# Stage B of a spectral filter on 64x32 and 32x64 array tiles, with each filter row stored once

## The chip, the core and the metric

One core of one Trainium2 chip runs the whole program. It has TensorE (PE, matmuls, which reads SBUF and writes PSUM), VectorE (DVE), ScalarE (ACT), GpSimd (POOL), SyncE (SP, here only an issuer of DMAs) and 16 DMA engines that all issuers share. PSUM has eight banks of 128 x 512 fp32. The metric is the device time of one execution in microseconds (us); it is the same for every engine, and the last engine to finish sets it.

## The reference

```python
def _attn_ref(x, filt_r, filt_i):          # x (8, 3008, 256), filters (1505, 256)
    X = np.fft.rfft(x, axis=1)
    Y = X * (filt_r + 1j * filt_i)[None, :, :]
    return np.fft.irfft(Y, n=x.shape[1], axis=1).astype(np.float32)

def _moe_ref(x, w_gate, w_val, w_out):     # x (24064, 256), d_ff 1536
    gate = np.maximum(x @ w_gate, 0.0)
    val = x @ w_val
    return (gate * val @ w_out).astype(np.float32)
```

The output of the first is the input of the second. All inputs and the output are fp32.

## The kernel before, in words

**The transform.** The 3008 positions of a batch are split as 94 x 32. Stage A transforms along the 94 (a matmul with a constant matrix; `a_0` and `a_1` for batches 0 and 1, `tiled_a` on 32x32 array tiles for batches 2 to 7). Stage B transforms along the 32, multiplies by the filter and transforms back along the 32. Stage C (`item_c`) transforms back along the 94 and yields `yT`, 512 tokens at a time. Then comes the feed-forward part (`gv`, `o_part`).

**Stage B before.** The 48 row groups of a batch are handled in six steps i. `fwd(b, i)` issues 8 matmuls on 64x64 array tiles (four at once) into two PSUM banks psX; `product(b, i, e, k)` multiplies one bank by the real filter (k = 0, result `tt`) or the imaginary one (k = 1, result `uu`) on DVE; in batch 0, eight of the `uu` are made on POOL from a copy `xs` that ACT takes out of PSUM first. `inv(b, i)` issues 16 matmuls on 64x64 tiles into two banks psD, with constant tables I2t for `tt` and I2u for `uu`; ACT copies both banks out (DVE one in batch 0). The result goes to DRAM (`Dbuf`), in batch 0 to SBUF. A 64-row tile holds the real parts of a group in 32 rows and the imaginary parts in 32 more, and both halves are multiplied by the same filter row: the filter tables Ftr and Fti (24 groups x 256) hold each row twice. The tables are loaded by POOL's DMAs (`load_filters`), and `place_filter` then copies 32 rows to the other 32, seven times by DMAs on SP's queue and once by POOL. Tables I2t come out of F2 by small matmuls (`make_back_t`), I2u out of I2t by a matmul with a swap matrix (`make_back_u`), with a few rows from a constant (`place_own`).

**The order of work.** It is written by hand; every engine runs its instructions in the order in which the program issues them. PSUM banks come from a first-in first-out list (`bank`, `done`), fixed when the program is built. The prologue is: x of batch 0 on the SP and ACT queues; filters on POOL, held back by `hold_gpsimd` until the first half of x is in; stage A of batch 0 (12 items after the first four), with the tables made beside the last of them; `first_b`, which is stage B of batch 0 with `amid(i)` between the steps (warm-up matmuls and `make_back_u` at i < 3, a stage-A item of batch 1 after that); the rest of stage A of batch 1. SP issues the filter copies, and x of batch 1 among and behind them.

Then come 47 blocks of 512 tokens, each of 12 steps. Step ft (its position in the block, 0 to 11) is `gv` (psV and psG, two matmuls each; ACT casts psV to `vsb`, DVE makes `prod` of psG and `vsb`), `o_part` of the block before (four psO matmuls, ACT's copy `osb` at positions 5 and 11), then whatever `at_step` has put on this step, then at positions 8 and 10 `item_c` of the next block, one half each. The half of position 8 is cast to `yT` by ACT, that of position 10 by DVE. The next block's first psV needs the first half for its first matmul and the second half for its second. `at_step` spreads the batches' work: for batch b, `end` is the step (always position 3) before whose neighbourhood its stage C begins, and the offsets in the code count from it. `turn_1(k)` are three DVE transposes of batch 1 in the first two blocks.

Of the kernel before, what the change touches and what calls it, by code (L numbers as in the profile page):

```python
# [40 lines left out]

def _tables():
# [9 lines left out]
    own = np.zeros((128, 2, 2, 64))  # L52
    for hg in range(48):
        g, a = divmod(hg, 2)
        rows = slice(a * 64, a * 64 + 64)
        e, j = g % 2, 12 * a + g // 2
# [4 lines left out]
        k1 = 1 + g + 24 * a if hg != 47 else 0  # L61
        th = 2 * np.pi * (((n1 - 23) * k1) % N1) / N1
        wa[part, rt] = np.cos(th)
        if k1 not in (0, 47):
# [5 lines left out]
            conj = np.tile([1.0, -1.0], 16)  # L70
# [3 lines left out]
            ct, st = c.T, s.T  # L74
            t[:] = np.block([[ct, st], [-st, ct]])
            u[:] = np.block([[-st, ct], [-ct, -st]]) * np.concatenate([conj, conj])[:, None]
        else:
# [9 lines left out]
            if k1 == 0:  # L87
                sign = np.where(n2 % 2 == 0, 1.0, -1.0)
                f[0:32, 32] = sign
                t[0, 0:32] = 1.0  # L90
                t[32, 0:32] = sign
                u[0] = 0.0
                u[32] = 0.0
        f2[lo + 64 * e, j] = f
        if g >= NG - 2:
            own[rows, 0, g - NG + 2], own[rows, 1, g - NG + 2] = t, u
# [4 lines left out]
    swap = np.zeros((128, 128))  # L101
    conj = np.where(r % 2 == 0, 1.0, -1.0)
    swap[r ^ 32, r] = conj * np.where(r & 32, -1.0, 1.0)
    fold = np.zeros((128, 4, 32))
    i = np.arange(24)
    for odd in range(2):
        k1 = 2 - odd + 2 * (i % 12) + 24 * (i // 12)
        if not odd:
            k1[k1 == 48] = 0
        th = 2 * np.pi * (np.outer(i - 23, k1) % N1) / N1  # L110
        half = np.where(i == 23, 0.5, 1.0)[:, None]
        for q in range(4):
            fold[32 * q:32 * q + 24, 2 * odd, 0:24] = np.cos(th) * half
            fold[32 * q:32 * q + 24, 2 * odd + 1, 0:24] = np.where(k1 % 47 == 0, 0.0, -np.sin(th))
    tab = np.concatenate([perm, swap, own.reshape(128, -1), m1.reshape(128, -1)], 1)
# [4 lines left out]
def kernel(  # L120
# [57 lines left out]
    I2t = consts.tile([128, NG, 64], BF16)  # L178
    I2u = consts.tile([128, NG, 64], BF16)
    Ftr = consts.tile([128, NG, D], BF16)  # L180
    Fti = consts.tile([128, NG, D], BF16)
# [18 lines left out]
    perm, swap = tabs[:, 0:64], tabs[:, 64:192]  # L200

    def make_back_t(q):

        psI = [bank("psI", 4, 64) for _ in range(2)]
        for e in range(2):
            for a in range(2):
                for j in range(4):
                    nc.tensor.matmul(psI[e][64 * a:64 * a + 64, j],
                                     F2[64 * e:64 * e + 64, 12 * a + 4 * q + j, :],
                                     perm[64 * e:64 * e + 64], start=True, stop=True,  # L210
                                     tile_position=(64 * e, 64 * a))
        for e in range(2):
            nc.scalar.copy(I2t[:, 8 * q + e:8 * q + 8:2, :], psI[e])
            done(psI[e])

    def make_back_u(q):

        psI = bank("psI", 8, 64)
        nc.tensor.matmul(psI, swap, I2t[:, 8 * q:8 * q + 8, :], start=True, stop=True)
        nc.scalar.copy(I2u[:, 8 * q:8 * q + 8, :], psI)  # L220
        done(psI)

    def place_own():

        for i, t in enumerate((I2t, I2u)):
            o = 192 + i * 128
            nc.gpsimd.tensor_copy(t[64:, NG - 2:, :],
                                  tabs[64:, o:o + 128].rearrange("p (g n) -> p g n", g=2))

    nyq = []  # L230

    def load_filters():

        for g0 in (0, H):
            for src, dst in FILT:
                for a in range(2):
                    r, k1, n = a * 64, 1 + 24 * a + g0, H - (2 * a if g0 else 0)
                    nc.gpsimd.dma_start(dst[r:r + 31:2, g0:g0 + n, :],
                                        _ap(src, k1 * D, [[N1 * D, 16], [1, n * D]]))
                    nc.gpsimd.dma_start(dst[r + 1:r + 32:2, g0:g0 + n, :],  # L240
                                        _ap(src, (N1 - k1) * D, [[N1 * D, 16], [-D, n], [1, D]]))
            yield

    def load_own_filters():
        for src, dst in FILT:
            nc.gpsimd.dma_start(dst[64:95:2, NG - 2:, :],
                                _ap(src, 47 * D, [[N1 * D, 16], [-47 * D, 2], [1, D]]))
            nyq.append(pro.tile([1, D], BF16, tag="nyq", bufs=2, name="nyq"))
            nc.gpsimd.dma_start(nyq[-1], _ap(src, (S // 2) * D, [[D, 1], [1, D]]))

    def place_filter(fi, a, half, copy):

        dst = FILT[fi][1]
        gs = slice(H * half, H * half + H)
        r = a * 64
        copy(dst[r + 32:r + 64, gs, :], dst[r:r + 32, gs, :])

    def place_nyq():
        for (src, dst), n in zip(FILT, nyq):
            nc.gpsimd.tensor_copy(dst[96:97, NG - 1, :], n)  # L260
# [141 lines left out]
    psXs, tus, dsbs, left = {}, {}, {}, {}  # L402
    CUTS = (0, 2, 4, 6)

    def fwd(b, i):
# [4 lines left out]
        for m in range(2):  # L410
            for e in range(2):
                for a in range(2):
                    j = 12 * a + 2 * i + m
                    nc.tensor.matmul(psXs[b, i, e][64 * a:64 * a + 64, m],  # L414
                                     F2[64 * e:64 * e + 64, j, :],
                                     ats[b][64 * e:64 * e + 64, j, :] if b > 1 else ats[b][64 * e:64 * e + 64, :, j, :],
                                     start=True, stop=True, tile_position=(64 * e, 64 * a))

    def product(b, i, e, k, pool=False):

        psX = psXs[b, i, e]
        pool_, bufs = (fs, 4) if b else (pro, 6)
        p = pool_.tile([128, 2, D], BF16, tag=("tt", "uu")[k], bufs=bufs, name=("tt", "uu")[k])
        filt = (Ftr, Fti)[k][:, 4 * i + e:4 * i + 4:2, :]
# [11 lines left out]
    def inv(b, i):  # L436

        if b and i in CUTS:
            dsbs[b] = i, sb.tile([128, 2, 4, D], BF16, tag="dsb", bufs=3, name="dsb")
        psD = [bank("psD", 2, D) for a in range(2)]  # L440
        for m in range(2):
            for k in range(2):
                for a in range(2):
                    for e in range(2):
                        nc.tensor.matmul(psD[a][64 * e:64 * e + 64, m],  # L445
                                         (I2t, I2u)[k][64 * a:64 * a + 64, 4 * i + 2 * m + e, :],
                                         tus[b, i, e, k][64 * a:64 * a + 64, m],
                                         start=(k == 0), stop=(k == 1),
                                         tile_position=(64 * a, 64 * e))
        if b:  # L450
            i0, dsb = dsbs[b]
            o = 2 * (i - i0)
        for a in range(2):
            copy = nc.vector.tensor_copy if (b, i, a) == (0, 5, 0) else nc.scalar.copy
            copy(dsb[:, a, o:o + 2, :] if b else DS0[:, 12 * a + 2 * i:12 * a + 2 * i + 2, :], psD[a])  # L455
            done(psD[a])
        if b and i + 1 in CUTS:
            for q in range(4):
# [278 lines left out]
```

## Time and profile before

| | |
|---|---|
| times of three runs | 878.98, 879.57, 881.71 us (median 879.57) |
| span of the profiled execution | 878.4 us |
| that execution's own time | not given beside its span; the three times lie 0.6 to 3.3 us above it |
| PE, DVE, ACT, POOL busy | 868.5, 576.5, 500.7, 364.3 us |
| granted TensorE clock | 1.00 throughout |
| first psV matmul of block 0 | 50.1 us |
| stage B of batch 0 on PE | 25.0 to 39.2 us |

"Busy" is the time in which an engine executes. A line of the chain gives a start, a length and what the chain did then. A line of the timeline gives a start, a length, the engine, the source line, the operation, output and inputs, sizes, a count, and in brackets how long the engine had been idle before it and on whom it waited. The length of a PE row with a count is from the first start to the last modelled end; successive rows overlap, so the step of PE is read from start to start.

### The profile page before, as it was taken

The page shows a single profiled execution, that of the slowest core. Times are in us where ns is not written, and L with a number is a line of the kernel's source. Part 1 is how long each engine was busy: PE and PEld are TensorE (multiplying, and loading weights), DVE is VectorE, ACT ScalarE, POOL GpSimd, SP SyncE. Part 2 cuts the span into 40 slices and gives each one's busy share as a digit, 9 for nine tenths or more (in the row PEclk, how much of TensorE's full clock was granted, in tenths as well). Part 3 has the DMA queues.
Part 4 walks back from the last instruction along what each step waited for, and adds up shares of the span by engine and source line. Part 5 has one row for each costly group of instructions (what it writes and reads, how often), then busy time and mean ns, then how long its engine had stood idle before and what let it go on. Part 6 is the DMA issues. An engine that isn't in the chain of part 4 may idle for free.

```text
span 878.4 us, 19202 instructions
## 1 busy us (share of the span) xinstructions
PE 868.5 (99%) x7184; PEld 507.4 (58%) x7184; DVE 576.5 (66%) x863; ACT 500.7 (57%) x905; POOL 364.3 (41%) x367
## 2 busy tenths in 40 slices
PE   8899999999999999999999999999999999999998
PEld 3445655666555665556655665556655656666665
DVE  4787766667666776567665777657766577655553
ACT  4865655565555656555655565555565555555553
POOL 7718940166901688017870287603884000000001
PEclk9999999999999999999999999999999999999999
DMA  9996454634754347634475344663445512421111
GB/s 251 239 179 110 133 140 106 128 93 102 187 120 101 105 109 181 132 92 101 119 190 114 83 117 126 166 126 88 124 134 141 119 40 69 98 60 36 38 32 53
DMA packets 107075, 102.85 MB, mean 117 GB/s; under 512 B 24216, under 2 KB 92344, under 8 KB 106215
## 3 DMA queue, kind: packets, MB, share of 16 engines
q1 hardware_dynamic: 83974, 74.45, 34.7%
q0 software_dynamic: 22608, 26.41, 13.0%
q8 instruction: 56, 0.92, 0.5%
q10 hardware_dynamic: 400, 0.79, 0.3%
q14 instruction: 37, 0.29, 0.1%
HBM read 58.16 MB, written 45.88 MB: 118 GB/s over the span
## 4 chain that ended last, share of the span: by engine, by line
PE 95%; DMA 3%; POOL 1%; DVE 1%; ACT 0%; issue 0%; SPq 0%; DVEq 0%; POOLq 0%
PE psV L526 29%; PE psG L526 28%; PE psO L547 27%; PE psF L377 3%; PE psY L509 2%; PE psD L445 2%; PE psX L414 2%; PE psA L284 2%; DMA Fti<-Fti 1%; DMA XF<-in_x_dram 1%; DMA Fti<-in_filt_i_dram 1%; POOL out_dram L571 0%; DMA out_dram<-XF 0%; DVE uu L430 0%; DVE prod L531 0%
## 5 line engine op out<-in xcount | busy, mean ns | idle before, releaser
L531 DVE SCALAR_TENSOR_TENSOR prod<-psG,vsb 128x512 bf16<-128x512 f32 x564 | 388.4, 689 | 256.2 <-ACT vsb L529 250.1
L529 ACT CAST vsb<-psV 128x512 bf16<-128x512 f32 x564 | 331.9, 589 | 262.8 <-PE psV L526 171.1
L526 PE MATMUL psV<-yT,WvT 128*128 128x512 bf16 x1128 | 336.7, 379 | 0.6 <-DVE yT L517 0.6
L547 PE MATMUL psO<-WoT,prod 128*128 128x256 bf16 x2256 | 336.5, 273 | 0.0
L526 PE MATMUL psG<-yT,WgT 128*128 128x512 bf16 x1128 | 335.3, 379 | 0.0
L547 PEld LDWEIGHTS <-prod 128*128 128x128 bf16 x2256 | 220.7, 98 | 143.4
L526 PEld LDWEIGHTS <-WgT 128*128 128x128 bf16 x1128 | 110.0, 98 | 134.5 <-issue 1.5
L276 POOL CAST scr<-prod 128x8 f32<-128x8 bf16 x24 | 4.5, 189 | 284.5 <-DVE prod L531 284.5
L526 PEld LDWEIGHTS <-WvT 128*128 128x128 bf16 x1128 | 98.3, 98 | 41.4 <-issue 30.2
L571 POOL DMA_DIRECT2D out_dram<-osb x5 | 2.7, 535 | 200.1 <-ACT osb L560 200.0
L560 ACT COPY osb<-psO 128x512 f32<-128x512 f32 x92 | 53.9, 586 | 25.9 <-PE psO L547 23.8
L430 DVE TENSOR_TENSOR tt<-psX,Ftr 128x512 bf16<-128x512 f32 x96 | 64.8, 680 | 0.9 <-PE psX L414 0.5
L430 DVE TENSOR_TENSOR uu<-psX,Fti 128x512 bf16<-128x512 f32 x88 | 59.8, 680 | 1.9 <-DMA Fti<-Fti 1.9
L363 POOL TENSOR_TENSOR fold<-XF 128x1024 f32<-128x1024 f32 x24 | 57.6, 2401 | 3.7 <-DMA XF<-in_x_dram 3.0
L350 POOL DMA_DIRECT2D XF<-in_x_dram x96 | 56.7, 596 | 3.7 <-PE psY L509 1.5
L364 POOL TENSOR_TENSOR XF<-XF 128x1024 f32<-128x1024 f32 x24 | 56.4, 2350 | 1.9
L455 ACT CAST dsb<-psD 128x512 bf16<-128x512 f32 x84 | 45.1, 589 | 11.0 <-PE psD L445 11.0
L384 DVE CAST asb<-psF 128x512 bf16<-128x512 f32 x48 | 30.9, 686 | 17.8 <-PE psF L377 17.8
L384 ACT CAST asb<-psF 128x512 bf16<-128x512 f32 x48 | 25.8, 589 | 29.0 <-PE psF L377 29.0
L515 ACT CAST yT<-psY 128x512 bf16<-128x512 f32 x47 | 27.5, 586 | 23.1 <-PE psY L509 23.0
L509 PE MATMUL psY<-M,dCb 96*128 96x94 bf16 (+19 forms) x604 | 37.5, 198 | 0.0
L509 PEld LDWEIGHTS <-dCb 96*128 96x128 bf16 (+1 forms) x604 | 34.5, 97 | 3.3 <-issue 0.8
(69 smaller groups left out, 472.2 us busy)
## 6 DMA issues: line engine op xcount, KB each, us to landing
XF<-in_x_dram POOLq DMA_DIRECT2D x48, 256.0 KB, 6.2
Dbuf<-dsb SPq DMA_DIRECT2D x84, 128.0 KB
dCb<-Dbuf SPq DMA_DIRECT2D x56, 192.0 KB
XF<-in_x_dram POOLq DMA_DIRECT2D x96, 96.0 KB, 2.7
Abuf<-asb SPq DMA_DIRECT2D x96, 96.0 KB
at<-Abuf SPq DMA_DIRECT2D x24, 384.0 KB
out_dram<-osb SPq DMA_DIRECT2D x69, 94.0 KB
XF<-in_x_dram SPq DMA_DIRECT2D x20, 256.0 KB
```

What stands on the lines that cost most here:

```text
L350: nc.gpsimd.dma_start(xp[r:r + 24, 0:4:2, :], _ap(x, (b * N1 * N2 + o) * D, [[N2 * D, 24], [47 * N2 * D, 2], [1, 512]]))
L363: tt(t, xp[:, 0:2], xp[:, 2:4], op=ALU.add)
L364: tt(xp[:, 2:4], xp[:, 0:2], xp[:, 2:4], op=ALU.subtract)
L384: copy(asf[:, :, q, :], banks[q])
L430: nc.vector.tensor_tensor(p, psX, filt, op=ALU.mult)
L455: copy(dsb[:, a, o:o + 2, :] if b else DS0[:, 12 * a + 2 * i:12 * a + 2 * i + 2, :], psD[a])
L509: nc.tensor.matmul(psY[:, o:o + w], dCs[b, n2 // 8][:, n2 % 8, h * 128:(h + 1) * 128], M1[:, 1, n1:n1 + w] if b == 0 else M1[:NROW, 0, n1: ...
L526: nc.tensor.matmul(pt[:, :W], w[:, h, ft * 128:(ft + 1) * 128], yt[:, h, :], start=(h == 0), stop=(h == 1))
L529: nc.scalar.copy(vsb, psV[:, :W])
L531: nc.vector.scalar_tensor_tensor(prod, in0=psG[:, :W], scalar=0.0, in1=vsb, op0=ALU.max, op1=ALU.mult)
L547: nc.tensor.matmul(psO[:, t % 2], prods[ft][:, t * 128:(t + 1) * 128], WoT[:, ft, :], start=(ft == 0), stop=(ft == NFT - 1))
L560: copy(osb[:, t0 % 2:t % 2 + 1], psO[:, t0 % 2:t % 2 + 1])
```

## The change

- `fwd` issues 16 matmuls of half the width on 64x32 tiles (eight at once); groups are renumbered (`_k1`) so that one PSUM bank holds real parts and imaginary parts in its two halves (r), on the same partitions. `product` therefore reads one filter row for both halves (a zero stride).
- Ftr and Fti shrink to 12 groups; `place_filter`, its copies and `place_nyq` go. `load_filters` issues 24 DMAs instead of 16. The POOL hold ahead of it waits on the second quarter of XF[0] instead of its end.
- `inv` takes two groups at a time: 64 matmuls on 32x64 tiles (eight at once) into four banks, four copies (ACT; in batch 0's last, DVE two).
- `make_back_t` makes 48 + 48 smaller matmuls instead of 16 + 16 + 16; I2u is made by two POOL operations.
- x of batch 1 is issued behind a small DMA (`hold`) that waits on Fti rows 96 and 97.
- `at_step` offsets move: `turn_1`, `tiled_a`, `fwd` (two at once), `product`, `inv`.

```diff
-    def make_back_u(q):
-        psI = bank("psI", 8, 64)
-        nc.tensor.matmul(psI, swap, I2t[:, 8 * q:8 * q + 8, :], start=True, stop=True)
-        nc.scalar.copy(I2u[:, 8 * q:8 * q + 8, :], psI)
-        done(psI)
+    def make_back_u():
+        for r in range(2):
+            nc.gpsimd.tensor_scalar(I2u[:, r], I2t[:, 1 - r], conj[:, r:r + 1], 1.0, op0=ALU.mult, op1=ALU.mult)
...
+        for src, dst in FILT:
+            for c in range(4):
+                load_back(src, dst, c, 0, H // 2)
+            for c in range(4):
+                r, k1, n = 32 * c, 1 + H * c, H - c // 3
+                nc.gpsimd.dma_start(dst[r:r + 31:2, :n, :], _ap(src, k1 * D, [[N1 * D, 16], [1, n * D]]))
+        for src, dst in FILT:
+            for c in range(4):
+                load_back(src, dst, c, H // 2, H - c // 3)
+
+    def load_back(src, dst, c, g0, g1):
+        r, k1 = 32 * c + 1, 1 + H * c + g0
+        nc.gpsimd.dma_start(dst[r:r + 31:2, g0:g1, :],
+                            _ap(src, (N1 - k1) * D, [[N1 * D, 16], [-D, g1 - g0], [1, D]]))
...
     def fwd(b, i):
...
-        for m in range(2):
-            for e in range(2):
-                for a in range(2):
-                    j = 12 * a + 2 * i + m
-                    nc.tensor.matmul(psXs[b, i, e][64 * a:64 * a + 64, m],
-                                     F2[64 * e:64 * e + 64, j, :],
+        for r in range(2):
+            for c in range(4):
+                for e in range(2):
+                    j = 4 * i + c
+                    nc.tensor.matmul(psXs[b, i, e][32 * c:32 * c + 32, r],
+                                     F2[64 * e:64 * e + 64, j, 32 * r:32 * r + 32],
                                      ats[b][64 * e:64 * e + 64, j, :] if b > 1 else ats[b][64 * e:64 * e + 64, :, j, :],
-                                     start=True, stop=True, tile_position=(64 * e, 64 * a))
+                                     start=True, stop=True, tile_position=(64 * e, 32 * c))
...
-        filt = (Ftr, Fti)[k][:, 4 * i + e:4 * i + 4:2, :]
+        filt = (Ftr, Fti)[k][:, 2 * i + e, :]
+        filt = dataclasses.replace(filt, ap=[list(filt.ap[0]), [0, 2], list(filt.ap[1])])
...
+    def inv(b, q):
+
+        psD = [bank("psD", 2, D) for c in range(4)]
         for m in range(2):
             for k in range(2):
+                for r in range(2):
+                    for c in range(4):
+                        for e in range(2):
+                            i = 2 * q + m
+                            nc.tensor.matmul(psD[c][64 * e:64 * e + 64, m],
+                                             (I2t, I2u)[k][32 * c:32 * c + 32, r, 2 * i + e, :],
+                                             tus[b, i, e, k][32 * c:32 * c + 32, r],
+                                             start=(k == r == 0), stop=(k == r == 1),
+                                             tile_position=(32 * c, 64 * e))
+        dst = sb.tile([128, 8, D], BF16, tag="dsb", bufs=3, name="dsb") if b else DS0[:, 8 * q:8 * q + 8, :]
+        for c in range(4):
+            copy = nc.vector.tensor_copy if not b and q == 2 and c < 2 else nc.scalar.copy
+            copy(dst[:, c:8:4, :], psD[c])
+            done(psD[c])
...
-            if i > 1:
-                inv(0, i - 2)
             amid(i)
-        inv(0, 4)
-        amid(6)
-        inv(0, 5)
+            if i in (3, 4):
+                inv(0, i - 3)
+        inv(0, 2)
...
-    hold_gpsimd(XF[0][:, 4 * q - 8:])
+    hold_gpsimd(XF[0][:, 2 * q - 8:2 * q])
...
-    place_filter(1, 0, 0, nc.gpsimd.tensor_copy)
-    for fi, a, half in ((0, 0, 0), (0, 1, 0), (1, 1, 0), (0, 0, 1), (0, 1, 1)):
-        place_filter(fi, a, half, nc.sync.dma_start)
-    load_x(1, sp, ((0, 0, 2 * q),))
-    for a in range(2):
-        place_filter(1, a, 1, nc.sync.dma_start)
-    load_x(1, sp, ((0, 2 * q, 4 * q), (1, 0, 2 * q), (1, 2 * q, 4 * q)))
+    hold = sb.tile([2, 8], BF16, tag="hold", bufs=1)
+    nc.sync.dma_start(hold, Fti[96:98, 4, 0:8])
+    load_x(1, sp, ((0, 0, 2 * q), (0, 2 * q, 4 * q), (1, 0, 2 * q), (1, 2 * q, 4 * q)))
...
-        at_step((4, 11, 14)[k - 1], lambda k=k: turn_1(k))
+        at_step((4, 9, 12)[k - 1], lambda k=k: turn_1(k))
...
-            for j, e in enumerate((-74, -69, -64, -57)):
+            for j, e in enumerate((-72, -67, -62, -57)):
...
-        for i in range(7):
-            l = -35 + 5 * i if b == 1 else -40 + 6 * i
-            if i < 6:
+        for z in range(3):
+            l = (-37, -25, -13)[z] if b == 1 else -44 + 14 * z
+            for i in (2 * z, 2 * z + 1):
                 at_step(end + l, lambda b=b, i=i: fwd(b, i))
                 for h in range(4):
-                    at_step(end + l + h, lambda b=b, i=i, h=h: product(b, i, h // 2, h % 2))
-            if i > 0:
-                at_step(end + l, lambda b=b, i=i: inv(b, i - 1))
+                    at_step(end + l + i % 2 * 4 + h, lambda b=b, i=i, h=h: product(b, i, h // 2, h % 2))
+            at_step(end + l + (9 if b == 1 else 10) - (z == 2), lambda b=b, z=z: inv(b, z))
```

## The prediction

> **What bounds the kernel now.** I read the page first (busy times, chain), then the chain in order of time over the first 62 us, then PE, ACT, DVE and POOL instruction by instruction in the windows that the change touches. From the page:
>
> ```profile
> PE 868.5 (99%) x7184; PEld 507.4 (58%) x7184; DVE 576.5 (66%) x863; ACT 500.7 (57%) x905; POOL 364.3 (41%) x367
> PE 95%; DMA 3%; POOL 1%; DVE 1%; ACT 0%; issue 0%; SPq 0%; DVEq 0%; POOLq 0%
> ```
>
> TensorE sets the end, so a saving elsewhere counts only where PE waits. PE waits in the prologue. The chain of 0 to 62 us:
>
> ```profile
> 20.02 5.87 DMA Fti<-Fti
> ...
> 28.09 4.53 DMA Fti<-Fti
> 32.62 0.03 issue
> 32.65 0.05 DVEq L430
> 32.70 0.04 issue
> 32.74 0.70 DVE uu L430
> ...
> 38.66 0.56 PE psD L445 x16
> 39.23 9.64 PE psA L284 x22
> ```
>
> Both filter copies that the change removes stand in this chain; stage B of batch 0 ends at 39.23. Behind it PE runs 11 stage-A items of batch 1 back to back, 0.876 us each.
>
> PE in a later batch, and three rows that price small matmuls and waits (the 0.35 us row is batch 0's table transposition; 79.58 is step 24, the first of the third block):
>
> ```profile
> 20.69 0.35 PE L208 MATMUL psI<-tabs,F 64*64 64x64 bf16 x16
> 79.58 0.38 PE L526 MATMUL psV<-yT,WvT 128*128 128x512 bf16 x1 [0.39 <-DVE yT L517]
> 221.55 0.60 PE L547 MATMUL psO<-WoT,prod 128*128 128x256 bf16 x4
> 222.08 0.30 PE L445 MATMUL psD<-tt,I2t 64*64 64x256 bf16 x4
> 222.22 0.28 PE L445 MATMUL psD<-uu,I2u 64*64 64x256 bf16 x4
> 222.32 0.28 PE L445 MATMUL psD<-tt,I2t 64*64 64x256 bf16 x4
> 222.43 0.28 PE L445 MATMUL psD<-uu,I2u 64*64 64x256 bf16 x4
> 222.65 0.60 PE L526 MATMUL psV<-yT,WvT 128*128 128x512 bf16 x2
> 225.35 1.14 PE L377 MATMUL psF<-XF,WF 24*32 24x512 f32 x32
> ```
>
> A plain step (psV 0.435, psG 0.435, psO 0.435) takes 1.30 us. A round of four tile matmuls takes 0.109; going to the tiles and back costs 0.09 before, 0.03 in the first round and 0.10 after: 0.22 a visit. ACT and DVE on each other's heels:
>
> ```profile
> 205.13 1.07 ACT L455 CAST dsb<-psD 128x512 bf16<-128x512 f32 x2 [0.19 <-PE psD L445]
> 220.40 0.69 DVE L531 SCALAR_TENSOR_TENSOR prod<-psG,vsb 128x512 bf16<-128x512 f32 x1 [0.56 <-ACT vsb L529]
> 221.01 0.68 DVE L517 CAST yT<-psY 128x512 bf16<-128x512 f32 x1
> 26.22 5.79 POOL L428 TENSOR_TENSOR uu<-xs,Fti 128x512 bf16<-128x512 f32 x5 [2.35 <-ACT xs L427]
> ```
>
> ACT starts one every 0.48 when queued, DVE every 0.61, POOL's product every 1.16. In that step psV began at 219.16, so prod starts 1.24 after psV.
>
> **1. Stage B's matmuls, batches 1 to 7.** Twice as many, each on half a tile, twice as many at once: forward 16 x 0.109/8 x 2 groups = 4 rounds a visit, inverse 64/8 = 8 rounds. Per batch 36 rounds before and after. Visits fall from 7 (six forwards, five of them with an inverse, and the last inverse) to 6. No row shows eight tiles. Bounds: with the visit unchanged, 7 x 0.25 = 1.7 us less. psF has 16 tiles; its two passes (0.43 each) with return take 1.07, 0.21 over the streaming against 0.13 for psD: with that a visit costs 0.30 and 6 cost 0.25 more than 7 did: 1.8 more. Eight lie between: visit 0.25, 7 x (7 x 0.22 - 6 x 0.25) = 0.3 less. I take **-0.3**.
>
> **2. yT behind the products.** The old forwards of batches 2 to 7 began at position 11 or 5 of the block, so none of their four products fell on position 10, where DVE also casts the next block's yT. Now eight products follow two forwards begun at positions 7, 9 and 11; the first two sets cover position 10. There, from psV: prod 1.24, product 1.85, yT 2.46 to 3.14. The next block's second psV matmul would start after two steps, psY (0.24) and one matmul: 1.30 + 0.24 + 1.30 + 0.22 = 3.06, so it waits 0.13. Two sets in six batches: **+1.6** (0, if DVE gains 0.13 anywhere; 3.2, if a late vsb doubles it). Batch 1 had this at steps 24 and 36 (0.55 and 0.14, first psV matmul to second, less 0.22); its new positions avoid it: **-0.7**.
>
> **3. Four psD copies ahead of yT.** The third inverse of batches 2 to 7 stands at position 8, ahead of the first yT half; before, inverses stood at 5 and 11 with two copies. From psV of that step: matmuls 1.40, last round 2.18, copies from 2.49 (0.31 later, as at 213.50 to 213.81) at 2.49, 2.97, 3.45, 3.93; queued behind on ACT: yT 4.41, vsb of steps 9 and 10 at 4.89 and 5.37. DVE: prod 5.51 and 6.12, yT 6.73 to 7.41. PE needs it at 6.99: it waits 0.46. Six times: **+2.8** (0, if ACT is as far behind as now, two copies less; 5.4, if a queued copy takes its whole 0.59). The first two inverses (5 and 7) leave time to recover. PSUM covers the rest: four psX banks leave three for psV and psG, each freed 0.4 us or more before its turn. With that cover gone a late step would add its lateness to each of eight.
>
> **4. turn_1 earlier.** Transposes of batch 1 move from steps 11 and 14 to 9 and 12. The one at step 9 (1.20, next start 1.10) now stands ahead of prod and yT of step 10 on DVE. Before: prod 59.42, prod 60.23, yT 60.84 to 61.52, PE at 61.57. After: transpose 60.03, prod 61.1, yT 61.7 to 62.4: **+0.9**. The half of `at` read from HBM has landed by 60; forward moves only from step 16 to 14, near 65.
>
> **5. Prologue.** Removed: seven filter copies on SP's queue and one on POOL (2.73), three swap matmuls. Added: 48 table matmuls, eight filter DMAs (POOL issues 0.5 to 0.57 each), two tensor_scalar operations on POOL, one more item behind stage B (12 instead of 11).
> - The filters' hold releases on x's second quarter, about 1.5 us earlier; they share DMA with x's last quarter, already at 270 to 360 GB/s. I put x 0.5 later, and the 48 table matmuls that now stand ahead of the last stage-A item (16 before) 0.3: stage B starts at 25.8 instead of 25.0.
> - POOL waits on its eighth-last DMA as now; its issues end near 21.5. I2t is copied by 24.4. The tensor_scalars handle 768 elements: at the copy's rate (3072 in 2.73) about 0.8 each, at the two-input rate (1024 in 2.4) 1.8. One tensor input, so nearest the copy: 0.85. With own tables (0.7) POOL's products start at 26.8.
> - Six products at 1.16: 33.75. The second inverse needs the sixth; its copies start at 34.2 on ACT, and the last xs copy is queued behind four of them: 36.1 to 36.7. Last product 36.8 to 37.9, last inverse to 38.3. That is 0.95 earlier than 39.23, less the extra item's 0.88: **-0.1**. The removed copies' wait is replaced by POOL and ACT.
> - Bounds: tensor_scalar at 1.8 each: +1.8. If only PE counted: from 22.0 to 39.2 its rows (forwards 2.0, inverses 2.9, four items 3.5, warm-up 3.3, swaps 0.7, tables 0.3) leave 4.5 idle; with the swaps -5.2.
> - x of batch 1: its hold opens when 16 filter DMAs have landed, near 21.6; issue 22.2 instead of 24.5. First use is near 30; if late, it adds directly.
>
> Filter rows read twice by a zero stride cost DVE nothing: shape and PSUM input stay. Dbuf stores are as many, in 4 KB rows. `at` loads land at 160 for a forward now at 169, then at 165.
>
> **Sum:** -0.3 + 1.6 - 0.7 + 2.8 + 0.9 - 0.1 = +4.2 on the span of 878.4. The median shown, 879.57, stands 1.2 above that span: 883.8.
>
> **Rivals.**
> *Matmul pitch (8%).* If 27 ns (0.109/4) were PE's pitch and not streaming, 1152 more matmuls cost 31 us: 915. Against it: 16 psI in 0.35, of which the last lasts 0.19, start 11 ns apart; eight in 0.109 need 13.6. That margin is thin: at 16 ns, 36 rounds x 0.02 x 8 batches = 6 more: 890. It decides from 13.6 ns up.
> The Trainium skill, TensorE: Matmul & The Clock Gate, section "Wait — 56ns, not 53.3ns?", says that starts never come closer than about 25 ns; by that, as an estimate, the kernel would take some 910. The 11 ns row disagrees.
> *Prologue PE-bound (15%), not slower.* The copies were the only thing in the way, and POOL and ACT keep up: -5.2 instead of -0.1 gives 878.7. It decides from about -4.3. For it: DVE idles 1.9 before uu at 32.74. Against: POOL's eight products at 1.16 fill 26.8 to 36.1 alone.
> *Filters delay x, or I2u delays POOL (17%).* Stage B starts 2 us later: 885.8. For it: DMA is busy above 90% from 5 to 27 us.
>
> **Chances.** Mine 60%: own range 881.5 to 886. About 0.3% (2.6 us) is what a measurement here tells from no change: 876.9 to 882.2 is "same". A sixth of mine and most of the PE-bound case lie there; beyond it to the fast side only if the waits of 2 and 3 also fail to appear. Faster 0.06, same 0.24, slower 0.70. Range 879.5 to 888.5.
>
> **What would show it.** Step 1: psD eight rounds near 0.11, 6 visits. Steps 2 to 4: start to start of the two psV matmuls in a block's first step, 0.22 without a wait: 0.35 (twice) and 0.68 (once) in each of batches 2 to 7, near 1.5 at step 12. Step 5: last inverse of batch 0 near 38.3 behind a POOL uu. Wrong if psD rounds exceed 0.12, if those stay at 0.22, or if the first psV leaves 49.5 to 51.5 us.

## The result and the profile after

The changed kernel takes 884.74 us (median of 5 runs, 882.56 to 885.25) against 880.36 us before (5 runs on the same chip, 878.98 to 881.71): a ratio of 1.0046, with a 95% interval of 1.0033 to 1.0059: slower by half a per cent, clear of the noise. The profiled execution has a span of 883.0 us against 878.4, so 4.6 us are to be accounted for.

The page of the changed kernel: busy times, the chain's shares by engine, and the largest group of psV matmuls (busy, mean ns of one, idle before them and on whom):

```profile
PE 869.7 (98%) x8381; PEld 508.5 (58%) x8381; DVE 577.4 (65%) x864; ACT 493.6 (56%) x899; POOL 365.7 (41%) x374
PE 92%; DMA 3%; DVE 2%; ACT 2%; issue 1%; POOL 1%; ACTq 0%; DVEq 0%
L505 PE MATMUL psV<-yT,WvT 128*128 128x512 bf16 x1128 | 338.6, 379 | 2.9 <-DVE yT L496 2.9
```

PE is busy for 1.2 us more, with 1197 more matmuls; its share of the chain falls from 95% to 92%, and ACT, DVE and "issue" take what it loses. Most of the loss is therefore PE waiting.

The chain in order of time, through stage B of batch 0 and to the wait at step 12 (start, length, what the chain did):

```profile
13.53 5.52 DMA Fti<-in_filt_i_dram
...
22.92 3.75 DMA Fti<-in_filt_i_dram
...
33.39 0.67 PE psD L428 x36
34.06 0.85 issue
34.90 0.61 PE psD L428 x25
35.51 0.44 ACT AS L436
35.97 1.57 ACT AS L436 x3
37.55 0.50 ACT xs L410
38.11 1.17 POOL uu L411
39.32 0.42 PE psD L428 x16
39.74 10.50 PE psA L267 x24
50.24 0.47 PE psY L488 x12
...
62.95 0.69 DVE yT L496
63.69 0.38 PE psV L505
```

The filter copies are gone. In their place stand ACT (four copies, then xs behind them) and POOL, as predicted; but ahead of them PE itself stops for 0.85 us in the middle of the second inverse, behind no semaphore (the line "issue"). Stage B ends at 39.74 instead of 39.23, and 12 items follow instead of 11.

PE's timeline at the first step of the second block (63.69), at a pair of forwards (206.21) and at a double inverse (218.57):

```profile
63.69 0.38 PE L505 MATMUL psV<-yT,WvT 128*128 128x512 bf16 x1 [1.00 <-DVE yT L496]
...
206.21 0.63 PE L396 MATMUL psX<-at,F 64*32 64x256 bf16 x32
206.77 0.60 PE L505 MATMUL psV<-yT,WvT 128*128 128x512 bf16 x2
...
218.57 0.42 PE L428 MATMUL psD<-tt,I2t 32*64 32x256 bf16 x16
218.81 0.40 PE L428 MATMUL psD<-uu,I2u 32*64 32x256 bf16 x16
219.03 0.40 PE L428 MATMUL psD<-tt,I2t 32*64 32x256 bf16 x16
219.25 0.40 PE L428 MATMUL psD<-uu,I2u 32*64 32x256 bf16 x16
219.58 0.41 PE L488 MATMUL psY<-M,dCb 96*128 96x50 bf16 x6
```

Start to start, 32 forward matmuls and the return take 0.56 us (four rounds of 0.109 are 0.44), 64 inverse matmuls and the return 1.01 us (eight rounds are 0.87). A round of eight tiles thus lasts as long as a round of four did, and an excursion to the tiles costs 0.12 to 0.14 on either count, with the 0.09 of the entry ahead of it some 0.22, as before.

The wait of a block's first step is read from PE's starts: first to second psV matmul, less the 0.2165 us of an undisturbed pair. At the third inverse of batch 2, for example, 0.72 less 0.2165 is a wait of 0.50:

```profile
223.96 0.38 PE L505 MATMUL psV<-yT,WvT 128*128 128x512 bf16 x1
224.68 0.38 PE L505 MATMUL psV<-yT,WvT 128*128 128x512 bf16 x1 [0.34 <-DVE yT L496]
```

These waits, and the steady part from the first psV matmul of the program to the last, give the budget (us):

| | before | after | difference |
|---|---|---|---|
| first psV matmul starts | 50.11 | 51.49 | +1.38 |
| wait at step 12 | 0.42 | 1.16 | +0.74 |
| waits at steps 24 and 36 | 0.55, 0.14 | none | -0.69 |
| waits in batches 2 to 7 | none | 4.36 (twelve of 0.11 to 0.14, six of 0.45 to 0.51) | +4.36 |
| rest of the steady part (817.57 before, 820.70 after) | | | -1.28 |
| from the last psV to the end | 10.68 | 10.77 | +0.09 |

The sum is +4.6. The rest of the steady part, -1.28, is what is left over when the waits are taken out; one excursion is saved in each of batches 1 to 7, which makes it 0.18 for each, where 7 x 0.22 would be 1.5.

### The profile page after: what moved, and what is told of

Same layout as the page of the kernel before. It is cut to its first block, busy times and chain, and to the rows that moved or that the text cites. A ratio compares the mean times of both kernels' runs of the same rounds, so it can differ in the third digit from the quotient of the medians.

```text
span 883.0 us, 21560 instructions
## 1 busy us (share of the span) xinstructions
PE 869.7 (98%) x8381; PEld 508.5 (58%) x8381; DVE 577.4 (65%) x864; ACT 493.6 (56%) x899; POOL 365.7 (41%) x374
## 4 chain that ended last, share of the span: by engine, by line
PE 92%; DMA 3%; DVE 2%; ACT 2%; issue 1%; POOL 1%; ACTq 0%; DVEq 0%
PE psV L505 28%; PE psO L526 27%; PE psG L505 27%; PE psF L360 3%; PE psD L428 3%; PE psY L488 2%; PE psA L267 1%; PE psX L396 1%; DMA Fti<-in_filt_i_dram 1%; ACT dsb L436 1%; DMA XF<-in_x_dram 1%; DMA Ftr<-in_filt_r_dram 1%; DVE yT L496 1%; DVE tt L413 0%; DVE prod L510 0%
## 5 line engine op out<-in xcount | busy, mean ns | idle before, releaser
L539 ACT COPY osb<-psO 128x512 f32<-128x512 f32 x92 | 53.9, 586 | 25.8 <-PE psO L526 25.0
L436 ACT CAST dsb<-psD 128x512 bf16<-128x512 f32 x84 | 43.1, 600 | 19.9 <-PE psD L428 19.9
L367 ACT CAST asb<-psF 128x512 bf16<-128x512 f32 x48 | 25.8, 589 | 34.6 <-PE psF L360 34.6
```

The lines of the kernel that those rows point to most:

```text
L367: copy(asf[:, :, q, :], banks[q])
L436: copy(dst[:, c:8:4, :], psD[c])
L539: copy(osb[:, t0 % 2:t % 2 + 1], psO[:, t0 % 2:t % 2 + 1])
```

## The experiments

Two theories were to be tested. Of the steady part: that the waits come from where products, inverses and transposes stand in the block, and can be moved away. Of the prologue, where the prediction had missed: what stops PE in the second inverse, and what the earlier filters do to x. Each ratio below is to the kernel before, timed anew on the same chip (880.05 to 880.69 us).

### The third inverse one step earlier

In batches 2 to 7 the third inverse moves from position 8 to 7, so that its copies are no longer just ahead of the first yT half.

```diff
-            at_step(end + l + (9 if b == 1 else 10) - (z == 2), lambda b=b, z=z: inv(b, z))
+            at_step(end + l + (9 if b == 1 else 10) - (z == 2) - (z == 2 and b > 1), lambda b=b, z=z: inv(b, z))
```

> The changed kernel with one edit: the third inverse of batches 2 to 7 stands at position 7 of the block instead of 8. Theory (the waits of 0.49 us at the first step of six blocks come from four psD copies queued on ACT ahead of the first yT half): those six waits go, the twelve of 0.13 stay, time 2.9 us lower, span near 880.1. Rival (the wait belongs to the inverse itself, eight rounds on 32-row tiles before the block's end, wherever it stands): the waits stay near 0.49 and the time within 0.5.

Measured: 881.91 us, a ratio to before of 1.0015 (1.0004 to 1.0026). The six waits near 0.49 are gone and the twelve short ones stay (1.45 in all); the steady part is 817.82, 2.88 less than in the changed kernel. Step 3 of the prediction (2.8) is shown, place and size. What makes the wait is asked below, with the kernel before.

### Forwards and inverses where no yT is cast

```diff
-            l = (-37, -25, -13)[z] if b == 1 else -44 + 14 * z
+            l = (-37, -25, -13)[z] if b == 1 else -40 + 12 * z
...
-            at_step(end + l + (9 if b == 1 else 10) - (z == 2), lambda b=b, z=z: inv(b, z))
+            at_step(end + l + (9 - (z == 2) if b == 1 else 8), lambda b=b, z=z: inv(b, z))
```

All forwards of batches 2 to 7 stand at position 11 and all inverses at 7.

> The changed kernel with the stage-B steps of batches 2 to 7 moved so that all three sets begin at position 11 (products at 11 and 0 to 6) and all inverses stand at 7; tiles and copies as in the changed kernel. Theory (position, not tiles): all 18 waits before the second psV matmul in batches 2 to 7 go (4.4 us in sum), span near 878.6, about level with the kernel before. Rival (the smaller tiles or the four-bank inverses cost time themselves): less than 2 us comes back.

Measured: 880.44 us, ratio 0.9997 (0.9985 to 1.0008). No wait is left in batches 2 to 7, the steady part is 816.23, 4.47 less than in the changed kernel and 1.34 less than before. PE's waits from 64 to 875 us, of the changed kernel (total, times, longest):

```profile
PE psV L505 <- DVE yT L496: 2.9, 7, 1.0
```

and of this one, where only step 12 is left:

```profile
PE psV L505 <- DVE yT L496: 1.0, 1, 1.0
```

(This view counts the idle time of PE, which is less than the delay from start to start, and leaves out the shortest waits.)

### The transposes back

```diff
-        at_step((4, 9, 12)[k - 1], lambda k=k: turn_1(k))
+        at_step((4, 11, 12)[k - 1], lambda k=k: turn_1(k))
```

> The changed kernel with the second and third later transposes of batch 1 at steps 11 and 12 instead of 9 and 12. Theory: the wait of psV at step 12 falls from 1.16 back to about 0.4 (before: 0.42), time 0.7 us lower. Rival (the wait comes from the prologue's later end, which shifts DVE and ACT alike): it stays above 1.0.

Measured: 884.27 us, ratio 1.0047 (1.0033 to 1.006). The wait at step 12 is 0.42 again and the steady part 819.96, 0.74 less. The time did not follow, since the first psV of the profiled execution came at 53.01 instead of 51.49: the prologue moves by more than this repair from execution to execution. Step 4 is shown by its wait. DVE's timeline of the changed kernel:

```profile
60.80 0.69 DVE L510 SCALAR_TENSOR_TENSOR prod<-psG,vsb 128x512 bf16<-128x512 f32 x1 [0.46 <-ACT vsb L508]
61.41 1.08 DVE L294 STREAM_TRANSPOSE at<-asb 128x512 f32<-128x512 f32 x1
62.39 0.65 DVE L510 SCALAR_TENSOR_TENSOR prod<-psG,vsb 128x512 bf16<-128x512 f32 x1
62.95 0.68 DVE L496 CAST yT<-psY 128x512 bf16<-128x512 f32 x1
```

The transpose holds DVE for 0.98 us from start to start, with the next block's yT two places behind it.

### The kernel before with the new positions

The kernel before (four 64x64 tiles, doubled filter rows, its own prologue), with forwards, products, inverses, `tiled_a` and `turn_1` of batches 1 to 7 at the changed kernel's steps:

```diff
-        for i in range(7):
-            l = -35 + 5 * i if b == 1 else -40 + 6 * i
...
+        for z in range(3):
+            l = (-37, -25, -13)[z] if b == 1 else -44 + 14 * z
+            for i in (2 * z, 2 * z + 1):
+                at_step(end + l, lambda b=b, i=i: fwd(b, i))
+                for h in range(4):
+                    at_step(end + l + i % 2 * 4 + h, lambda b=b, i=i, h=h: product(b, i, h // 2, h % 2))
+                at_step(end + l + (9 if b == 1 else 10) - (z == 2), lambda b=b, i=i: inv(b, i))
```

> The kernel before (64x64 tiles, doubled filter rows, its own prologue) with the changed kernel's positions in batches 1 to 7: two forwards at one step, eight product steps, two inverses together at the step of the double inverse, and the new steps of tiled_a and turn_1. Theory: steps 2 to 4 of the prediction come from the positions alone, whatever the tiles. Then the waits of a block's first step are as in the changed kernel (about 4.4 us in batches 2 to 7, 1.16 at step 12, none at 24 and 36), the visits to the array tiles are 6 a batch instead of 7 (-1.3 us), and the first psV stays near 50.1 us: from first to last psV +3.1 over before (817.6), the time some 883.5 to 884. Rival: the narrow tiles themselves (slower copies or products out of banks with two halves, or dearer visits) cost in the steady part: then the waits are clearly below 4.4 us and the time is within 1.5 us of before.

Measured: 881.44 us, ratio 1.0012 (1.0004 to 1.0021); steady part 818.24, only 0.67 over before. The twelve short waits are there (0.11 to 0.14), and step 12 has 1.27; but the third inverse's wait is 0.08 instead of 0.49 (two of its six places can't be read, for missing records). So the theory as written fell: the positions alone make 2 of the 4.4 us. ACT at the third inverse of batch 2, in this kernel, whose first psD matmul starts at 218.07:

```profile
218.73 2.05 ACT L455 CAST dsb<-psD 128x512 bf16<-128x512 f32 x4 [0.84 <-PE psD L445]
220.65 0.63 ACT L515 CAST yT<-psY 128x512 bf16<-128x512 f32 x1
```

and in the changed kernel, where it starts at 218.57:

```profile
219.67 2.05 ACT L436 CAST dsb<-psD 128x512 bf16<-128x512 f32 x4 [1.28 <-PE psD L428]
221.59 0.63 ACT L494 CAST yT<-psY 128x512 bf16<-128x512 f32 x1
```

The copies last the same. They begin 0.66 behind the first matmul here and 1.10 there: two 64x64 inverses finish two banks after half of the visit, while the double inverse writes all four banks to the end, so that ACT starts late and ends late, yT too (2.58 and 3.02). The difference of 0.44 is the wait's, 0.41. The time fell where the rival had it, but not by the rival's mechanism: the copies are no slower, and the visit lasts 1.00 here and 1.01 there. The rows point to the bank order of the double inverse as the rest of the cost; a double inverse that finishes its banks one after the other was not run.

### More visits

The rephased kernel, with the second forward of each pair one step later: 21 more visits in batches 1 to 7.

```diff
-                at_step(end + l, lambda b=b, i=i: fwd(b, i))
+                at_step(end + l + i % 2, lambda b=b, i=i: fwd(b, i))
```

> e2_rephase with the second forward of each pair one step later, so that three more visits to the array tiles are made in each of batches 1 to 7: 21 more. Theory: a visit costs 0.22 us, as it did with four tiles: from first to last psV 4.6 us more than in e2_rephase (816.2), 820.8. Rivals: a visit with eight tiles is dearer, the 0.25 that the prediction took or 0.30: 5.3 or 6.3 us more; or the entry and the return overlap with neighbours and it costs under 0.1: 2 us more or less.

Measured: 884.63 us, ratio 1.0038 (1.0023 to 1.0054); steady part 821.07, with the wait at step 12 as the only wait on yT, as in the rephased kernel. That is 4.84 more for 21 visits, 0.23 each: the visit costs with eight tiles what it cost with four, and the prediction's 0.25 was slightly too dear.

### POOL's last product on DVE

```diff
-    POOL_U = ((0, 1), (1, 0), (1, 1), (2, 0), (2, 1), (3, 1), (4, 0), (5, 0))
+    POOL_U = ((0, 1), (1, 0), (1, 1), (2, 0), (2, 1), (3, 1), (4, 0))
```

> The changed kernel with the last POOL product of batch 0 (group 5) made by DVE, so that no xs copy queues behind the four psD copies of the second inverse. Theory (POOL and ACT took the place of the filter copies as the end of stage B of batch 0): the last psD of batch 0 ends near 38.9 instead of 39.7, first psV 0.8 earlier than 51.5, time 0.8 lower. Rival (PE's own work bounds the stretch, or DVE becomes the end): less than 0.3.

Measured: 883.9 us, ratio 1.0039 (1.0027 to 1.0051). The last psD matmul starts at 38.87 instead of 39.48 and the first psV at 50.89 instead of 51.49. The steady part is unchanged (820.69). Stage B began 0.40 later in this execution, and PE stopped as in the changed kernel, for 0.96 instead of 1.11 us; from stage B's start to the first psV, less that stop, it takes 23.90 instead of 24.75. That is the 0.8 of the theory; the times alone do not resolve it (their intervals overlap).

### What stops PE in the second inverse

The stop is in most profiles of kernels with this prologue, at one place: behind the 100th psD matmul, in the middle of a round of eight. The four matmuls of the round that had started read the same two products as the four that had not. The records of the DMA engines show a 16 KB packet of PE's instruction queue shortly before it. (That the queue is PE's is read from its size: the pages count 66 such packets after the change and 56 before, and 16762 and 14368 loads and matmuls of PE, which is some 255 to a packet.) The changed kernel's DMA answer from 32.4 to 33.6 us:

```profile
q1 hardware_dynamic: 84, 0.43, 89.2%
q8 instruction: 1, 0.02, 4.9%
```

In it x of batch 1 takes 89% of the DMA engines' time; whether that makes the packet late was not tested. The next kernel leaves out the nine warm-up matmuls between the first three steps of stage B, 18 PE instructions with their weight loads; they compute nothing that is used.

```diff
         if i < 3:
-            warm(3)
+            pass
```

> The changed kernel without the nine warm-up matmuls between the first three steps of stage B of batch 0 (they compute nothing that is used). 18 PE instructions fewer stand ahead of the second inverse. In four of five profiles PE stopped 1 to 1.9 us in that inverse behind the same instruction, with no semaphore. Theory instruction supply: PE runs out of fetched instructions at a fixed place of its stream, so the stop moves to an instruction 18 later in program order. Rival: it is the data (a product or a copy that this instruction waits for and the records do not show); then the stop stays at the same instruction, the fifth matmul of the inverse's second half.

PE's timeline there:

```profile
34.94 0.42 PE L428 MATMUL psD<-tt,I2t 32*64 32x256 bf16 x16
35.18 0.40 PE L428 MATMUL psD<-uu,I2u 32*64 32x256 bf16 x16
35.40 0.39 PE L428 MATMUL psD<-tt,I2t 32*64 32x256 bf16 x13
36.46 0.30 PE L428 MATMUL psD<-tt,I2t 32*64 32x256 bf16 x3 [0.68 <-issue]
```

and the same place in the changed kernel:

```profile
33.32 0.42 PE L428 MATMUL psD<-tt,I2t 32*64 32x256 bf16 x16
33.56 0.40 PE L428 MATMUL psD<-uu,I2u 32*64 32x256 bf16 x16
33.78 0.28 PE L428 MATMUL psD<-tt,I2t 32*64 32x256 bf16 x4
34.90 0.41 PE L428 MATMUL psD<-tt,I2t 32*64 32x256 bf16 x12 [0.85 <-issue]
```

The stop moved from behind the 4th to behind the 13th matmul of the group: nine pairs later in the program, and at the same count of PE's instructions (the 690th load or matmul). Data or a copy would have held the same matmul. (The time of the one run, 886.22, says little: PE also waited 2.4 us for x of batch 1.)

The start of the packet, and the instruction behind that count, counted with the records that a trace lacks (us):

| | packet starts | 691st starts | between | stop of PE, start to start |
|---|---|---|---|---|
| changed kernel | 32.49 | 34.90 | 2.41 | 1.11 |
| third inverse earlier | 32.14 | 34.53 | 2.39 | 0.10 |
| rephased | 34.08 | 36.43 | 2.35 | 1.66 |
| transposes back | 34.01 | 36.42 | 2.42 | 1.89 |
| last product on DVE | 32.88 | 35.15 | 2.27 | 0.96 |
| no warm-up | 34.01 | 36.46 | 2.45 | 0.94 |
| hold back (below) | 33.82 | 36.02 | 2.20 | 1.62 |
| more visits | 33.35 | 35.71 | 2.36 | 1.19 |
| changed kernel again (below) | 35.12 | 37.51 | 2.39 | 1.45 |
| repaired version (below) | 31.91 | 35.28 | 3.37 | none |
| the same, last product on DVE (below) | 31.95 | 35.06 | 3.11 | none |
| new order of the inverses alone (below) | 33.03 | 35.86 | 2.83 | none |

In the profiles with a stop PE gets there 0.5 to 2.3 us after the packet's start and goes on 2.2 to 2.45 after it; in the three without, it gets there later than that and does not stop. The Trainium skill, Runtime: NRT & Kernel Launch, section "Instruction fetch mechanics", says that an engine's instructions are fetched in 16 KiB blocks of 256 while the block before runs, and that crossing a block is mostly hidden. The packet size agrees; that it is hidden does not hold here: 128 loads and matmuls of a double inverse take about 1.0 us, so PE would run through a block of 256 in about 2.0, faster than the 2.2 to 2.45 from a packet's start to PE's going on. What sets the moment at which the fetch begins, and what fills that time beyond the packet's own record of 0.95 us or less, is not shown.

### The filters' hold back

```diff
-    hold_gpsimd(XF[0][:, 2 * q - 8:2 * q])
+    hold_gpsimd(XF[0][:, 4 * q - 8:])
```

> The changed kernel with the filters' hold on POOL waiting for the end of XF[0] again, as before the change. Theory: the filters' DMAs, released at x's second quarter, share the DMA engines with x's last part and delay stage B by 0.6 to 1.5 us (it began at 25.6 to 26.5 in the five profiles with the change, at 25.0 before). Then stage B begins near 25.0 here, but POOL's eight products begin later by what the filter issues are late, some 1 us, and the time is within 1 us of the changed kernel. Rival: x is late for another reason (it differs from execution to execution): stage B begins at 25.6 or later here too.

Measured: 885.4 us, ratio 1.0058 (1.0042 to 1.0074). Stage B begins at 25.09, as before the change; in the eleven profiles with the earlier hold it begins at 25.63 to 27.90, median 26.36. What is gained there is lost again: the filters, and x of batch 1 behind them, come later, and PE waits for that x at the first stage-A item of batch 1:

```profile
30.29 1.10 PE L267 MATMUL psA<-XF,WA 128*128 128x512 f32 x2 [1.49 <-DMA XF<-in_x_dram]
```

The first psV comes at 52.61.

### A repaired version

Both repairs of the steady part, and in stage B of batch 0 the first two inverses one forward later, so that the xs copy of the last POOL product is no longer behind the second inverse's four copies:

```diff
-            amid(i)
-            if i in (3, 4):
-                inv(0, i - 3)
+            if i < 5:
+                amid(i)
+            if i > 3:
+                inv(0, i - 4)
+        amid(5)
         inv(0, 2)
```

(with the two edits of `l` and `inv` and that of `turn_1` from above)

> The two repairs of the steady part together (batches 2 to 7: forwards at position 11 of the block, inverses at 7; turn_1 at steps 4, 11, 12), and in stage B of batch 0 the first and second inverse one forward later, so that the last copy xs for POOL is not queued behind the second inverse's copies on ACT. Theory: the repairs add (-4.5 and -0.7), and the last product on POOL ends near 36.7 instead of 39.3, so that the first psV comes 1 to 2.5 us earlier than in the changed kernel: 877 to 878.7 us, below before (880.7). Rival: the prologue is set by PE's stop and by x, not by POOL's last product: then only the steady part counts, 879.5 us.

Measured: 877.59 us (7 runs), ratio 0.9970 (0.9959 to 0.9981): faster than before by 0.3%, and by the ratios 0.8% faster than the changed kernel. The steady part is 815.49, and 0.42 at step 12 is the only wait of a block's first step that its records show. PE's stop is gone, and the chain shows stage B as PE's own work, from the first inverse on but for two DVE products:

```profile
32.78 1.02 PE psD L428 x57
33.81 0.68 DVE uu L413
34.48 0.61 DVE tt L413
35.13 1.08 PE psD L428 x64
36.21 1.06 PE psA L267 x2
37.27 1.01 PE psD L428 x64
38.28 10.50 PE psA L267 x24
```

From this version, POOL's last product on DVE as well (the edit of `POOL_U` above):

> f4_late_inv with the last of POOL's products, (5,0), on DVE as well. Theory: with the copy xs out of the queue of the second inverse's copies, POOL's last product is no longer what the last inverse waits for, and DVE takes it at no gain: within 0.4 us of f4_late_inv (877.6). Rival: POOL's seven other products still end last: 0.6 to 1.1 us less, as in e4_uu5_dve.

Measured: 878.24 us, ratio 0.9971 (0.9962 to 0.9981): no gain, as the theory has it. From stage B's start to the first psV it takes 24.20 us, 0.3 more than in the repaired version. POOL's last product matters only while its xs copy is queued late.

### The new order of the inverses alone, and the changed kernel once more

The edit of stage B of batch 0 without the others; and the changed kernel, on the same chip.

> The changed kernel with only the order of stage B of batch 0 altered as in f4_late_inv (first and second inverse one forward later). Theory: the prologue's loss comes from PE's stop while its instructions are fetched (it ended 2.2 to 2.4 us after a 16 KB packet of the instruction queue began, in all six profiles that have it) and from the xs copy queued behind four copies; the new order takes away both, as in f4_late_inv: first psV 1.4 to 2 us earlier than in the changed kernel, steady part as there (820.7), 882.8 to 883.4 us. Rival: f4_late_inv's early first psV was its execution's luck with x: then 884.2 to 885 us here.

> The changed kernel once more, beside the three others on the same chip. Theory: the prologue differs from execution to execution by 1 to 2 us (first psV at 50.9 to 53.0 us in six profiles) and the steady part not at all: from first to last psV 820.7 within 0.1, PE's stop in the second inverse at the same instruction if its instructions' packet begins under 2.2 us before it is needed, and a median within 0.5 us of 884.7.

Measured: 884.51 us for the order alone, ratio 1.0036 (1.0024 to 1.0049); 885.09 for the changed kernel again, ratio 1.0051 (1.0037 to 1.0066). The stop is gone with the new order, and from stage B's start to the first psV it takes 23.87 us, as in the repaired version (23.88), against 25.86 and 26.20 in the two profiles of the changed kernel. But stage B itself began late in that execution, at 26.73, so the first psV came only 0.9 earlier than in the changed kernel's first profile, and the times differ by 0.6 us, with intervals that overlap. The mechanism is in the trace, but the time lies in the range of the rival (884.2 to 885), not of the theory (882.8 to 883.4): in the profile the late start of stage B took more than half of the gain back, and the gain in the time is not resolved. In the repeated profile of the changed kernel (one run 2 us above its median) stage B begins at 27.90, the first psV at 54.10, and the steady part is 820.69, the same to 0.01.

## Why the prediction was right or wrong

The forecast was 883.8 us, the time 884.74, inside the range and on the side that had most of the chance. Two of the steps were off, by 1.0 and 1.5 us, and cancelled for the most part: that the sum of the steps, +4.2, comes so near the measured +4.6 is in part luck. More than half of what is missing in the time itself comes from elsewhere. The forecast put the time 1.2 above the span, from a median and the span of another execution; in each run whose time and span are on record the time lies 1.7 or more above, in the changed kernel's five runs 1.74 to 1.78.

**1, tiles and visits (-0.3 taken, -1.3 measured): mis-sized.** The value lay between the bounds because psF's visit with sixteen tiles had looked dearer than psD's. The row with eight tiles goes with four: 0.22 to 0.23 a visit, in the profile after and by the 21 added visits. The bound with the visit unchanged was nearest. It was written as -1.7 with a visit of 0.25; with the working's own 0.22 it is -1.5.

**2, yT behind the products (+1.6 and -0.7): right.** Twelve waits of 0.11 to 0.14 make 1.45, steps 24 and 36 are clear (-0.69), and all twelve vanish when the forwards stand at 11.

**3, four copies ahead of yT (+2.8): right in size, 2.91 in six waits, and in place.** One sentence was too simple: that two copies more make the wait. The kernel before with the same four copies at the same position waits 0.08; by the rows above it is that all four banks are finished together, which the working used (copies begin 0.31 behind the last round) without naming it as the cause.

**4, turn_1 (+0.9): right, 0.74.** The transpose held DVE 0.98, where the working had 1.10.

**5, prologue (-0.1): wrong, +1.4.** The first psV came at 51.49, at the very edge of the stated 49.5 to 51.5; of the six profiles whose kernels leave this prologue as it is, four lie beyond, at 52.30 to 54.10. The chain behind it was the right one: the tensor_scalar operations took 0.90 each (0.85 taken), POOL's products began at 27.14 (26.8) and the sixth ended at 33.88 (33.75). The step that failed is the next one, "its copies start at 34.2 on ACT": they start at 35.49, and 1.1 of these 1.3 us is PE's stop in the second inverse, for instructions and not for data. No row of before shows such a stop; the sentence that bounded step 5 by "only PE counted" priced PE's rows as if instructions were always there. Without the stop the profiles are alike: first psV less stage B's start less the stop is 24.75 to 24.88 in the changed kernel's two profiles and in those of the third inverse earlier, rephased, transposes back and more visits, against 25.11 before (the same in the experiment with the new positions, whose prologue is that of before); and that with a 0.9 us item more. Step 5 had 24.2. The second part is stage B's start, 25.8 taken: 25.63 in this profile, but 26.36 as the median of eleven. The kernel before has 25.01, and its prologue in that experiment 25.82, so some 0.5 to 1.3 of it may be the earlier filters' cost; the single profile with the hold back, 25.09, agrees. That is three profiles against eleven, and their ranges overlap.

**The rivals.** *Matmul pitch* fell: 64 narrow matmuls and the return take 1.01 us, 15.8 ns each with everything, and PE's busy time grew by 1.2 us with 1197 more of them. The Trainium skill, TensorE: Matmul & The Clock Gate, section "Wait — 56ns, not 53.3ns?", has 25 ns as the least start to start; as an estimate that would be 1.6 us for these 64. The trace disagrees for matmuls on separate tiles, whose starts lie 3 to 4 ns apart within a round. *Prologue PE-bound* fell for the changed kernel, as POOL's xs is queued behind four copies and the last inverse waits for it; the repaired order shows that it was within reach in part: 23.9 from stage B's start to the first psV instead of 25.1. *Filters delay x* is probably true in its first half, at less than its 2 us; I2u delays nothing beyond its term.

## What to carry to other kernels

When more, smaller matmuls share the array at no cost in streaming, they still cost instructions: price a dense burst of them against the time from a block's fetch to PE's going on (2.2 to 2.45 us here), where nothing longer stands between. An operation that fills several PSUM banks had better finish them one after the other (the rows argue for it; it was not run), and stand where the engine that empties them has no deadline behind it; one step of the schedule was worth 2.9 us here. A prologue that moves by 1 to 2 us between executions is judged by differences within a profile (from one landmark to the next), not by one end time.

## What the runs showed of the hardware that was not expected

- PE can stop for lack of instructions, 0.94 to 1.89 us in eight profiles, at the same count of PE's instructions; it goes on 2.2 to 2.45 us after a 16 KB packet of its instruction queue starts. The profile calls it "issue".
- Eight tile matmuls (64x32 or 32x64, 256 columns) take the 0.109 us of four 64x64 ones, and changing between tiles and the whole array costs 0.22 to 0.23 us with these eight as with those four.
- The steady part repeats within 0.06 us between executions with the same steps (820.67 to 820.73 in six profiles), while stage B of the same prologue starts anywhere from 25.63 to 27.90.

What stays open: why the instruction packet begins when it does, why x lands differently from execution to execution, and why the repaired version gains some 1.6 us in the prologue by its times (6.8 us better than the changed kernel against before, of which 5.2 are steady) while the new order alone gained 0.6 to 1.3.
